# Shared value rows of an attention kernel: loaded once and copied on the chip, with one more load on a second DMA queue

## The chip, the cores and the metric

The kernel runs on one core of a Trainium2 chip. The metric is the device time of one execution in microseconds (us). All data are 32-bit floats.

The engines are named as in the profile: PE multiplies matrices (PEld is the loading of its weights), DVE works on vectors, ACT is the scalar engine, POOL is GpSimd, and SP issues DMAs. Each engine runs its instructions in the order of the program, and waits for others only through semaphores.

## The reference

Two parts follow each other. The first is chunked attention with memory: 4 batches, 8 heads, 768 positions, head size 64. Each chunk of 32 queries looks at 64 keys: 8 memory rows, 16 to the left, the 32 of the chunk and 8 to the right.

```python
for c in range(nc):                                  # 24 chunks of 32
    k_full = concat([mem_k, k[:, :, l_start:r_end]]) # 8 + up to 56 rows
    v_full = concat([mem_v, v[:, :, l_start:r_end]])
    scores = scale * q_c @ k_full.T
    a = exp(scores - max(scores)); a = a / (sum(a) + 1e-9)
    out[:, :, c_start:c_end] = a @ v_full
```

The second is a soft mixture of experts on the 3072 rows x of 512 numbers that come out: `logits = x @ phi` (32 slots, 4 for each of 8 experts); a softmax down the rows makes 32 slot inputs from x; each expert computes `relu(slot @ w1[e]) @ w2[e]`, with 2 MB of w1 and 2 MB of w2; and a softmax along the slots combines the 32 results into each row.

## The kernel before

**Tiles.** 128 positions, or 4 chunks, make a step u (24 of them), and two steps make a unit n (12 units, `NUNIT`). For a unit three things are loaded: q(n), 512 KB, and k(n), two transfers of 312 KB, into one of two slabs `kq0`, `kq1`; and v(n) into one of two slabs `v0`, `v1`. Heads go in pairs: the even partitions of k and v hold the first head of a pair, the odd ones the second (`par` in the code), and zeros stand in the halves of a slab that belong to the other head. For values the 64 rows that a chunk sees stand under each other, two partitions a row; a slab has one region for the first chunk of each two (`o` = 0) and one for the second (`o` = 1). The windows of the two chunks share 32 of their 64 rows, and these are loaded twice: v(n) is two transfers of 512 KB.

**A unit on PE.** The loop over n issues for each unit: transposes of the exponentials (`pt_ps`), the scores of the unit after it (`s`), logits (`l`) or transposes for the experts' softmax (`dt_ps`) in turn, a transpose of finished rows (`xt_ps`), the values of both steps (`a`), another `xt_ps`, and in each second unit `D_ps`, the slot sums. DVE and ACT do the softmax between `s` and `pt_ps`, ACT copies `pt`, `xT` and `dT` out of PSUM.

**The loads.** All DMAs are issued by SP, in order. In iteration n come q(n+3) and k(n+3) (when the scores that used the slab are done), then v(n+2) (when the values of unit n are done), then pieces of the experts' weights: 32 pieces of 1 MB, called w(0) to w(31) here. Twelve slabs `w0` to `w11` take the first twelve; further pieces go into kq, v and x slabs as the attention gives these up, and the last twelve into `w0` to `w11` again, each when PE has used the piece of w1 before it. `load_w(upto)` issues pieces up to a count; `n + 2` is the count in iteration n, and 11 from iteration 8.

**Semaphores of DMAs.** The layer that records the program gives each DMA one of eight semaphores, DMAHW0 to DMAHW7, in turn. A DMA waits until the DMA that had its semaphore before has landed. No more than eight DMAs are therefore on their way.

**After the attention** PE runs the eight experts' first product (`h`), then the second (`so`) in two blocks of 256 columns; each block is summed (`r`), combined into rows (`o`) and stored by six DMAs of 512 KB.

A small class sends every instruction through one helper, so that the profile shows L61 for nearly all of them; they are told apart by their tiles.

Of the kernel before, what the change touches and what calls it, by code (L numbers as in the profile page):

```python
# [16 lines left out]
P = 128  # L17
B, H, S, D = 4, 8, 768, 64
NPAIR = H // 2
CHUNK, LEFT, RIGHT, NMEM = 32, 16, 8, 8  # L20
NKEY = NMEM + LEFT + CHUNK + RIGHT
CPU = P // CHUNK
STEP = NMEM + 2 * CHUNK
UPB = S // P
NU = B * UPB
UU = 2
NUNIT = NU // UU
UNITS_B = UPB // UU
PAIRS = UU * CPU // 2
KW = PAIRS * STEP + LEFT + RIGHT  # L30
KB = NPAIR * KW
QW = UU * NPAIR * P
VB = UU * 2 * NPAIR * D
# [11 lines left out]
NEG = -1.0e30  # L45
PIECE = 2048
NW = 12
NIN = 2
# [18 lines left out]
def tile_attn_softmoe(  # L67
# [2 lines left out]
    qT: bass.AP,  # L70
    kT: bass.AP,
    vw: bass.AP,
    phi: bass.AP,
    w1: bass.AP,
    w2: bass.AP,
# [3 lines left out]
    pe, dve, act, sp, pool = (InOrder(tc, e) for e in (nc.tensor, nc.vector, nc.scalar, nc.sync, nc.gpsimd))  # L79
# [4 lines left out]
    kq_slab = [cp.tile([P, 2 * KB + QW], F32, tag=f"kq{i}", name=f"kq{i}") for i in range(NIN)]  # L84
# [8 lines left out]
    phi_sb = cp.tile([P, NKC, NSLOT], F32, tag="phi", name="phi_sb")  # L93
    warm = cp.tile([P, P], F32, tag="warm", name="warm")

    k_in = [t[:, 0:2 * KB].rearrange("p (a g n) -> p a g n", a=2, g=NPAIR) for t in kq_slab]
    q_in = [t[:, 2 * KB:].rearrange("p (u g n) -> p u g n", u=UU, g=NPAIR) for t in kq_slab]
    v_in = [t.rearrange("p a o (u c g d) -> p a o u c g d", u=UU, c=2, g=NPAIR) for t in v_slab]

# [8 lines left out]
    def load_kq(n):  # L108
        load_q(n)
        load_k(n)  # L110

    def load_v(n):
        t = v_slab[n % NIN]
        for par in range(2):
            sp.dma_start(t[par:P:2, par], vw[n, par])

    slabs = list(w_slab)
    usable = {i: NW for i in range(NUNIT + 2)}
# [15 lines left out]
    def load_w(upto):  # L134
        for i in range(len(where), min(upto, len(pieces))):
            kind, *at = pieces[i]
            where[pieces[i]] = s = slabs[i % len(slabs)]
            if kind == "w1":
                src = w1[at[0]].rearrange("(p kc) f -> p kc f", kc=NKC)[:, 2 * at[1]:2 * at[1] + 2, :]
                sp.dma_start(s.rearrange("p (k f) -> p k f", k=2), src)  # L140
            else:
                sp.dma_start(s, w2[at[0], at[1]])
# [12 lines left out]
    for i in range(NIN):  # L155
# [3 lines left out]
        out=kq_slab[1][:, 0:KB].rearrange("p (o n) -> p o n", n=104),  # L159
        in_=warm[:, 0:104].rearrange("p (o n) -> p o n", o=1).broadcast_to([P, KB // 104, 104]),  # L160
# [3 lines left out]
    for i in range(40):  # L164
        j = i % 4
# [15 lines left out]

    def scores(u):
        n, uu = divmod(u, UU)
        k, q = k_in[n % NIN], q_in[n % NIN]
        s_ps = ps.tile([P, H, NKEY], F32, tag="S", name=f"s{u}", bufs=2)
        for g in range(NPAIR):
            for j in range(CPU):
                w0 = (2 * uu + j // 2) * STEP + CHUNK * (j % 2)
                win = k[:, :, g, w0:w0 + NKEY]
                pe.matmul(  # L190
                    s_ps[32 * j:32 * j + 32, 2 * g:2 * g + 2, :],
                    lhsT=q[:, uu, g, 32 * j:32 * j + 32], rhs=win, start=True, stop=True,
                )
        return s_ps

    def softmax(u, s_ps):
        n, uu = divmod(u, UU)
        if u % UPB == 0:
            dve.memset(s_ps[0:32, :, 0:LEFT], NEG)
        if u % UPB == UPB - 1:  # L200
            dve.memset(s_ps[96:128, :, NKEY - RIGHT:NKEY], NEG)
        mx = wk.tile([P, H, 1], F32, tag="mx", name=f"mx{u}")
        dve.tensor_reduce(out=mx[:, :, 0], in_=s_ps, axis=AX.X, op=ALU.max)
        if uu == 0:
            pexp[n] = wk.tile([P, UU, NPAIR, NKEY, 2], F32, tag="p", name=f"p{n}")
        dve.tensor_tensor(
            out=pexp[n][:, uu].rearrange("p g n h -> p g h n"),
            in0=s_ps.rearrange("p (g h) n -> p g h n", h=2),
            in1=mx.rearrange("p (g h) o -> p g h o", h=2).broadcast_to([P, NPAIR, 2, NKEY]),
            op=ALU.subtract,  # L210
        )
        act.activation(out=pexp[n][:, uu], in_=pexp[n][:, uu], func=AF.Exp, scale=SCALE)

    def normalizer(n):
        z = wk.tile([P, UU, H], F32, tag="z", name=f"z{n}")
        zf = z.rearrange("p u h -> p (u h)")
        dve.tensor_reduce(
            out=z.rearrange("p u (g h) -> p (u g) h", h=2),
            in_=pexp[n].rearrange("p u g n h -> p (u g) h n"), axis=AX.X, op=ALU.add
        )  # L220
        dve.tensor_scalar_add(zf, zf, 1e-9)
        dve.reciprocal(out=zf, in_=zf)
        rz[n] = z

    def transpose_p(u):
        n, uu = divmod(u, UU)
        t_ps = ps.tile([P, NPAIR, P], F32, tag="T", name=f"pt_ps{u}", bufs=2)
        for g in range(NPAIR):
            pe.transpose(t_ps[:, g, :], pexp[n][:, uu, g].rearrange("p n h -> p (n h)"), ident)
        pt = wk.tile([P, NPAIR, P], F32, tag="pt", name=f"pt{u}", bufs=2)  # L230
        act.copy(out=pt, in_=t_ps)
        return pt
# [15 lines left out]
    def normalize(u, a_ps):  # L248
        n, uu = divmod(u, UU)
        dve.tensor_tensor(  # L250
            out=x_slab[u // 4 % 2][:, u % 4, :].rearrange("p (h d) -> p h d", d=D), in0=a_ps,
            in1=rz[n][:, uu].rearrange("p (h o) -> p h o", o=1).broadcast_to([P, H, D]), op=ALU.mult,
        )
# [103 lines left out]
    for u in range(UU):  # L357
        softmax(u, scores(u))
# [3 lines left out]
    for n in range(NUNIT):  # L362
        us = (2 * n, 2 * n + 1)
        last = n + 1 == NUNIT
        Gl = (n - 3) // 2 if n >= 3 and n % 2 == 1 else None
        Gd = (n - 4) // 2 if n >= 4 and n % 2 == 0 else None
        pts = [transpose_p(u) for u in us]
        if n >= 1:
            for u in us:
                normalize(u - 2, a_ps[u - 2])  # L370
        normalizer(n)
        if not last:
            s_ps = [scores(u + 2) for u in us]
        if n + 3 < NUNIT:
            load_kq(n + 3)
        if Gd is not None:
            dispatch_t(Gd)
        if Gl is not None:
            l_ps = logits(Gl)
        if n >= 1:  # L380
            transpose_x(us[0] - 2)
        if not last:
            for u, t in zip(us, s_ps):
                softmax(u + 2, t)
        if Gd is not None:
            combine_exp(Gd)
        if Gl is not None:
            dispatch_max(Gl, l_ps)
            dispatch_lT(Gl, l_ps)
            dispatch_exp(Gl, l_ps)  # L390
            if Gl >= 1:
                combine_div(Gl - 1)
        a_ps[us[0]] = values(us[0], pts[0])
        if last:
            transpose_x(us[1] - 2)
            normalize(us[0], a_ps[us[0]])
            dispatch_t(NG - 2)
        a_ps[us[1]] = values(us[1], pts[1])
        if n >= 1 and not last:
            transpose_x(us[1] - 2)  # L400
        if Gd is not None:
            D_ps = dispatch(Gd)
            dispatch_z(Gd)
            dispatch_sum(Gd, D_ps)
        if n + 2 < NUNIT:
            load_v(n + 2)
        load_w(usable[n] if n >= NUNIT - 3 else n + 2 + (n == NUNIT - 4))

    normalize(NU - 1, a_ps[NU - 1])
    transpose_x(NU - 2)  # L410
# [161 lines left out]
    sh = slot_out(0)  # L572
# [6 lines left out]
def _layouts(inputs):  # L579
    q, k, v = inputs["q"], inputs["k"], inputs["v"]  # L580

    def stream(x, mem):
        half = CHUNK // 2
        parts = [np.zeros((B, H, LEFT, D), x.dtype), x[:, :, :half]]
        for t in range(half, S, 2 * CHUNK):
            parts += [mem, x[:, :, t:t + 2 * CHUNK]]
        parts.append(np.zeros((B, H, RIGHT, D), x.dtype))
        return np.concatenate(parts, axis=2)

    qT = q.reshape(B, NPAIR, 2, UNITS_B, UU, P, D).transpose(0, 3, 6, 2, 4, 1, 5).reshape(NUNIT, P, QW)  # L590
    ks = stream(k, inputs["mem_k"])
    cols = np.array([[t * PAIRS * STEP + c for c in range(KW)] for t in range(UNITS_B)])
    kT = ks[:, :, cols].reshape(B, NPAIR, 2, UNITS_B, KW, D).transpose(0, 3, 2, 5, 1, 4).reshape(NUNIT, 2, D, KB)

    vs = stream(v, inputs["mem_v"])

    rows = np.array([[STEP * i + CHUNK * o + r for o in range(2) for r in range(NKEY)] for i in range(S // (2 * CHUNK))])
    vw = vs[:, :, rows].reshape(B, NPAIR, 2, UNITS_B, UU, 2, 2, NKEY, D).transpose(0, 3, 2, 7, 6, 4, 5, 1, 8)
    vw = vw.reshape(NUNIT, 2, NKEY, 2, VB)
    w2 = inputs["moe_w2"].reshape(E, NFC, P, NBLK, WB).transpose(3, 0, 2, 1, 4).reshape(NBLK, E, P, NFC * WB)  # L600
    return {"qT": qT, "kT": kT, "vw": vw, "phi": inputs["moe_phi"], "w1": inputs["moe_w1"], "w2": w2}


# [16 lines left out]
```

## Time and profile before

| | |
|---|---|
| time, median of 3 runs | 169.67 us (168.94 to 170.69) |
| the profiled execution | 170.3 us, of which the span of its instructions is 168.5 us |
| mean granted PE clock | 0.975 |
| PE, DVE, ACT, POOL busy | 139.9, 99.5, 60.4, 8.5 us |
| DMA packets | 66.84 MB, mean 397 GB/s |

The page lists for each engine how long it was busy, the span in 40 slices, the DMA queues, and the chain of work that ended last. The chain is followed back from the end: each row is a piece of work or a transfer that the next one waited for. In the list of waits a row names the engine and tile that waited, what released it, and the total, the number and the longest wait. "issue" there stands for a wait that the profile can't put down to any instruction or transfer.

### The profile page before, as it was taken

The numbers are of one execution on the slowest core, as the hardware profiler recorded it, in microseconds if no ns is written. First come the engines' busy times: TensorE is split into PE (matmuls) and PEld (weight loads), VectorE is DVE, ScalarE is ACT, GpSimd is POOL, SyncE is SP. The second block draws the span as 40 slices with busy tenths as digits, with TensorE's granted clock in tenths as the row PEclk, the third lists the DMA queues.
The fourth block names the chain that finished last, engine by engine and source line by source line (L and its number), as shares of the span: only waits on it lengthen the run. The fifth ranks groups of instructions, "written<-read, shape, count | busy, mean of one in ns | idle before, by whom it ended". The sixth has DMA issues, their size and how long they took to land.

```text
span 168.5 us, 6123 instructions
## 1 busy us (share of the span) xinstructions
PE 139.9 (83%) x2729; PEld 102.1 (61%) x2729; DVE 99.5 (59%) x216; ACT 60.4 (36%) x129; POOL 8.5 (5%) x13
## 2 busy tenths in 40 slices
PE   7369997895979979995995998889999999887800
PEld 6257885784758866884684766647655565553500
DVE  6566997974929994999498949466300101081620
ACT  5023543714532734371535455431122100070520
POOL 8700000000000000000000202000000000000000
PEclk9995999999999999999999999999999999999995
DMA  5999999999999999999999999999999999999896
GB/s 205 360 387 416 404 375 379 424 424 416 413 425 412 422 415 414 419 413 421 414 417 396 321 364 420 426 408 422 418 422 416 424 416 422 416 404 399 350 407 240
DMA packets 12458, 66.84 MB, mean 397 GB/s; under 512 B 2193, under 2 KB 2193, under 8 KB 6801
## 3 DMA queue, kind: packets, MB, share of 16 engines
q1 hardware_dynamic: 12432, 66.46, 97.1%
q8 instruction: 21, 0.34, 0.8%
q14 instruction: 5, 0.03, 0.0%
HBM read 60.16 MB, written 6.29 MB: 394 GB/s over the span
## 4 chain that ended last, share of the span: by engine, by line
PE 55%; DMA 22%; DVE 7%; issue 6%; POOL 3%; ACT 2%; DVEq 0%; ACTq 0%; POOLq 0%
PE s L61 13%; DMA w<-in_w_dram 12%; PE a L61 10%; PE xt_ps L61 6%; DMA kq<-in_kT_dram 6%; PE h L61 5%; PE pt_ps L61 4%; DMA kq<-in_qT_dram 4%; PE o L61 3%; PE D_ps L61 3%; PE l L61 3%; PE so L61 2%; POOL v L61 2%; PE dt_ps L61 2%; DVE v L61 1%
## 5 line engine op out<-in xcount | busy, mean ns | idle before, releaser
L61 PE MATMUL s<-kq 128*32 128x128 f32 x768 | 27.8, 294 | 6.7 <-issue 3.0
L61 PE MATMUL a<-v,pt 128*32 128x128 f32 x768 | 25.0, 274 | 4.9 <-issue 4.9
L61 PEld LDWEIGHTS s<-kq 128*32 128x32 f32 x768 | 23.1, 119 | 8.3 <-issue 4.9
L61 PEld LDWEIGHTS a<-v,pt 128*32 128x32 f32 x768 | 20.6, 110 | 8.0 <-issue 7.7
L61 ACT COPY xT<-xt_ps 128x512 f32<-128x512 f32 (+1 forms) x24 | 13.8, 576 | 28.4 <-PE xt_ps L61 28.4
L61 ACT ACTIVATE p<-p 128x512 f32<-128x512 f32 x24 | 14.7, 630 | 15.9 <-DVE p L61 15.9
L61 DVE TENSOR_TENSOR x<-a,z 128x512 f32<-128x512 f32 x24 | 15.6, 683 | 3.8 <-PE a L61 3.8
L61 DVE TENSOR_REDUCE mx<-s 128x8 f32<-128x512 f32 x24 | 16.3, 678 | 2.7 <-PE s L61 2.4
L61 DVE TENSOR_TENSOR p<-s,mx 128x512 f32<-128x512 f32 x24 | 16.7, 695 | 0.8
L61 PE MATMUL xt_ps<-ident,x 128*128 128x128 f32 x96 | 15.5, 284 | 0.0
L61 ACT COPY pt<-pt_ps 128x512 f32<-128x512 f32 x24 | 13.0, 590 | 5.5 <-PE pt_ps L61 5.5
L61 DVE TENSOR_REDUCE z<-p 128x16 f32<-128x1024 f32 x12 | 14.5, 1212 | 0.7 <-ACT p L61 0.7
L61 PE MATMUL pt_ps<-ident,p 128*128 128x128 f32 x96 | 13.3, 279 | 1.9 <-issue 1.2
L61 PEld LDWEIGHTS pt_ps<-ident,p 128*128 128x128 f32 x96 | 10.6, 141 | 6.0 <-ACT xT L61 3.4
L61 PEld LDWEIGHTS xt_ps<-ident,x 128*128 128x128 f32 x96 | 10.2, 140 | 4.0 <-issue 2.8
L61 PE MATMUL so<-w,hT 128*32 128x256 f32 x192 | 11.4, 381 | 0.5 <-DMA w<-in_w_dram 0.5
L61 PE MATMUL h<-w,siT 128*32 128x256 f32 x192 | 10.8, 380 | 0.1
L61 PE MATMUL o<-sh,cst 32*128 32x256 f32 x96 | 8.0, 404 | 1.6 <-DVE kq L61 0.6
L61 PEld LDWEIGHTS so<-w,hT 128*32 128x32 f32 x192 | 5.8, 110 | 5.5 <-DMA w<-in_w_dram 1.4
L61 DVE COPY hT<-ht_ps 128x32 f32<-128x32 f32 x8 | 1.2, 186 | 13.3 <-PE ht_ps L61 8.6
L61 PEld LDWEIGHTS h<-w,siT 128*32 128x32 f32 x192 | 6.0, 110 | 4.2 <-DVE siT L61 0.3
L61 PEld LDWEIGHTS o<-sh,cst 32*128 32x128 f32 x96 | 5.3, 184 | 4.3 <-DVE kq L61 1.4
(94 smaller groups left out, 133.5 us busy)
## 6 DMA issues: line engine op xcount, KB each, us to landing
w<-in_w_dram SPq DMA_DIRECT2D x24, 1024.0 KB, 11.8
v<-in_vw_dram SPq DMA_DIRECT2D x24, 512.0 KB, 9.3
kq<-in_kT_dram SPq DMA_DIRECT2D x24, 312.0 KB, 9.3
kq<-in_qT_dram SPq DMA_DIRECT2D x12, 512.0 KB, 9.6
v<-in_w_dram SPq DMA_DIRECT2D x4, 1024.0 KB, 9.8
out_dram<-v SPq DMA_DIRECT2D x8, 512.0 KB, 5.1
kq<-in_w_dram SPq DMA_DIRECT2D x2, 1024.0 KB, 10.1
x<-in_w_dram SPq DMA_DIRECT2D x2, 1024.0 KB, 8.5
```

Source lines behind the costliest of these rows:

```text
L61: return self.tc.keep_in_program_order(f(*args, **kwargs))
```

## The change

`load_v(n)` loads the rows of the first region alone (two transfers of 256 KB, `vw`), and for the second region only the 32 rows that are new (two transfers of 128 KB, `vx`). The new rows of the first head go on SP's queue, those of the second head on ACT's. The 32 shared rows are copied by POOL from the first region to the second, 64 partitions by 1024 numbers for each head. A copy stays on its partitions, so the order of the 64 keys in a chunk's window changes: for the second chunk the two halves of 32 are swapped, and the second head of a pair holds its keys in reverse, so that its shared rows lie in the other half of the partitions. The scores' matmul reads its keys through patterns that fit (two strides instead of one for second chunks), the masks of batch edges are set per head (two DVE memsets in place of one), and the order of rows on the host's side follows.

From iteration 4 on `load_w` goes one piece further than before, up to iteration 8, where both have issued 11.

```diff
     def load_v(n):
         t = v_slab[n % NIN]
         for par in range(2):
-            sp.dma_start(t[par:P:2, par], vw[n, par])
+            sp.dma_start(t[par:P:2, par, 0], vw[n, par])
+        for par in range(2):
+            (sp, act)[par].dma_start(t[65 * par:65 * par + 63:2, par, 1], vx[n, par])
+        for par in range(2):
+            shared = slice(64, P) if par == 0 else slice(0, 64)
+            pool.tensor_copy(out=t[shared, par, 1], in_=t[shared, par, 0])
...
     def scores(u):
...
-                win = k[:, :, g, w0:w0 + NKEY]
+                win = key_window(n, g, w0)
+                if j % 2:
+                    win = win.rearrange("p a (t i) -> p a t i", t=2)[:, :, ::-1, :]
...
     def softmax(u, s_ps):
         n, uu = divmod(u, UU)
+        sh = s_ps.rearrange("p (g h) n -> p g h n", h=2)
         if u % UPB == 0:
-            dve.memset(s_ps[0:32, :, 0:LEFT], NEG)
+            dve.memset(sh[0:32, :, 0, 0:LEFT], NEG)
+            dve.memset(sh[0:32, :, 1, NKEY - LEFT:NKEY], NEG)
...
-        load_w(usable[n] if n >= NUNIT - 3 else n + 2 + (n == NUNIT - 4))
+        load_w(usable[n] if n >= NUNIT - 3 else n + 2 + (n >= 4))
```

Below, V(n) stands for the two `vw` transfers of unit n, X(n) for the `vx` transfer on SP and A(n) for the one on ACT. With them a unit issues eight DMAs, and the semaphores fall to others than before. Three places of the program show what moved.

**SP in iteration 5** (q(8) and k(8) into kq0, v(7) into v1, then w). Before:

```order
L61 DMA kq0_64<-in_qT_dram 128x1024 [waits DMAHW5_49,PE_49]
L61 DMA kq0_64<-in_kT_dram 64x1248 [waits DMAHW6_49]
L61 DMA kq0_64<-in_kT_dram 64x1248 [waits DMAHW7_49]
L61 DMA v1_67<-in_vw_dram 64x2048 [waits DMAHW0_49,PE_49]
L61 DMA v1_67<-in_vw_dram 64x2048 [waits DMAHW1_49]
L61 DMA w6_76<-in_w1_dram 128x2048 [waits DMAHW2_49]
```

And now:

```order
L61 DMA kq0_64<-in_qT_dram 128x1024 [waits DMAHW6_49,PE_49]
L61 DMA kq0_64<-in_kT_dram 64x1248 [waits DMAHW7_49]
L61 DMA kq0_64<-in_kT_dram 64x1248 [waits DMAHW0_49]
L61 DMA v1_67<-in_vw_dram 64x1024 [waits DMAHW1_49,PE_49,Pool_49]
L61 DMA v1_67<-in_vw_dram 64x1024 [waits DMAHW2_49,Pool_49]
L61 DMA v1_67<-in_vx_dram 32x1024 [waits DMAHW3_49,PE_49]
L61 DMA w7_77<-in_w1_dram 128x2048 [waits DMAHW4_49]
```

The q(8) transfer has DMAHW6 now, which A(7) had before it. A(7) is issued by ACT at the end of this same iteration. In the same way q(9) follows A(8) in iteration 6, V(2) follows A(2) and V(3) follows A(3).

**ACT at the end of iteration 5** (xT9 is its copy of the last `xt_ps` of the iteration, pt12 and pt13 belong to the next):

```order
L61 COPY xT9_996<-xt_ps9_991 128x512 [waits PE_49]
L61 DMA v1_67<-in_vx_dram 32x1024 [waits DMAHW6_49]
L61 COPY pt12_1010<-pt_ps12_1005 128x512 [waits PE_49,Activation_49]
L61 COPY pt13_1017<-pt_ps13_1012 128x512 [waits PE_49,Activation_49]
L61 COPY dT1_1065<-dt_ps1_1062 128x128 [waits PE_49]
```

The DMA row, A(7), is new; what stands before and behind it stood there before. The semaphore that it waits for was A(6)'s.

**SP at iteration 9**, the last v load, v(11), and the first weights behind it. Before:

```order
L61 DMA v1_67<-in_vw_dram 64x2048 [waits DMAHW6_49,PE_49]
L61 DMA v1_67<-in_vw_dram 64x2048 [waits DMAHW7_49]
L61 DMA w11_81<-in_w1_dram 128x2048 [waits DMAHW0_49]
L61 DMA kq0_64<-in_w1_dram 128x2048 [waits DMAHW1_49]
L61 DMA kq1_65<-in_w1_dram 128x2048 [waits DMAHW2_49,PE_49]
```

And now:

```order
L61 DMA v1_67<-in_vw_dram 64x1024 [waits DMAHW5_49,PE_49,Pool_49]
L61 DMA v1_67<-in_vw_dram 64x1024 [waits DMAHW6_49,Pool_49]
L61 DMA v1_67<-in_vx_dram 32x1024 [waits DMAHW7_49,PE_49]
L61 DMA w11_81<-in_w1_dram 128x2048 [waits DMAHW0_49]
L61 DMA kq0_64<-in_w1_dram 128x2048 [waits DMAHW1_49]
L61 DMA kq1_65<-in_w1_dram 128x2048 [waits DMAHW2_49,PE_49]
```

X(11) has DMAHW7, which A(11) had before it; w(11) and all weights stand behind X(11) on SP.

More of the change, by code (lines that the diff above doesn't have):

```diff
@@ L72, in tile_attn_softmoe @@
     vw: bass.AP,
+    vx: bass.AP,
     phi: bass.AP,
@@ L94, in tile_attn_softmoe @@
     warm = cp.tile([P, P], F32, tag="warm", name="warm")
-    k_in = [t[:, 0:2 * KB].rearrange("p (a g n) -> p a g n", a=2, g=NPAIR) for t in kq_slab]
     q_in = [t[:, 2 * KB:].rearrange("p (u g n) -> p u g n", u=UU, g=NPAIR) for t in kq_slab]
@@ L114, in load_v, with key_window @@
         for par in range(2):
-            sp.dma_start(t[par:P:2, par], vw[n, par])
+            sp.dma_start(t[par:P:2, par, 0], vw[n, par])
[4 more added lines that the diff above has]
+            pool.tensor_copy(out=t[shared, par, 1], in_=t[shared, par, 0])
+    def key_window(n, g, w0):
+        t = kq_slab[n % NIN]
+        keys = t[:, g * KW + w0:g * KW + w0 + NKEY]
+        step = KB + KW - NKEY - 2 * w0
+        part, (one, count) = keys.ap[0], keys.ap[-1]
+        return bass.AP(tensor=keys.tensor, offset=keys.offset, ap=[part, [step, 2], [one, count]])
     slabs = list(w_slab)
@@ L183, in scores @@
         n, uu = divmod(u, UU)
-        k, q = k_in[n % NIN], q_in[n % NIN]
+        q = q_in[n % NIN]
         s_ps = ps.tile([P, H, NKEY], F32, tag="S", name=f"s{u}", bufs=2)
@@ L197, in softmax @@
         n, uu = divmod(u, UU)
+        sh = s_ps.rearrange("p (g h) n -> p g h n", h=2)
         if u % UPB == 0:
-            dve.memset(s_ps[0:32, :, 0:LEFT], NEG)
+            dve.memset(sh[0:32, :, 0, 0:LEFT], NEG)
+            dve.memset(sh[0:32, :, 1, NKEY - LEFT:NKEY], NEG)
         if u % UPB == UPB - 1:
-            dve.memset(s_ps[96:128, :, NKEY - RIGHT:NKEY], NEG)
+            dve.memset(sh[96:128, :, 0, CHUNK - RIGHT:CHUNK], NEG)
+            dve.memset(sh[96:128, :, 1, CHUNK:CHUNK + RIGHT], NEG)
         mx = wk.tile([P, H, 1], F32, tag="mx", name=f"mx{u}")
@@ L592, in _layouts, with rows @@
     cols = np.array([[t * PAIRS * STEP + c for c in range(KW)] for t in range(UNITS_B)])
-    kT = ks[:, :, cols].reshape(B, NPAIR, 2, UNITS_B, KW, D).transpose(0, 3, 2, 5, 1, 4).reshape(NUNIT, 2, D, KB)
+    kT = ks[:, :, cols].reshape(B, NPAIR, 2, UNITS_B, KW, D).transpose(0, 3, 2, 5, 1, 4)
+    kT = np.stack([kT[:, :, 0], kT[:, :, 1, :, :, ::-1]], axis=2).reshape(NUNIT, 2, D, KB)
     vs = stream(v, inputs["mem_v"])
-    rows = np.array([[STEP * i + CHUNK * o + r for o in range(2) for r in range(NKEY)] for i in range(S // (2 * CHUNK))])
-    vw = vs[:, :, rows].reshape(B, NPAIR, 2, UNITS_B, UU, 2, 2, NKEY, D).transpose(0, 3, 2, 7, 6, 4, 5, 1, 8)
-    vw = vw.reshape(NUNIT, 2, NKEY, 2, VB)
+    def rows(first, count):
+        r = np.arange(first, first + count)
+        at = np.array([[STEP * i + r, STEP * i + r[::-1]] for i in range(S // (2 * CHUNK))])
+        w = vs.reshape(B, NPAIR, 2, -1, D)
+        w = np.stack([w[:, :, par][:, :, at[:, par]] for par in range(2)], axis=2)
+        w = w.reshape(B, NPAIR, 2, UNITS_B, UU, 2, count, D).transpose(0, 3, 2, 6, 4, 5, 1, 7)
+        return w.reshape(NUNIT, 2, count, VB)
+    vw, vx = rows(0, 2 * CHUNK), rows(2 * CHUNK, CHUNK)
     w2 = inputs["moe_w2"].reshape(E, NFC, P, NBLK, WB).transpose(3, 0, 2, 1, 4).reshape(NBLK, E, P, NFC * WB)
-    return {"qT": qT, "kT": kT, "vw": vw, "phi": inputs["moe_phi"], "w1": inputs["moe_w1"], "w2": w2}
+    return {"qT": qT, "kT": kT, "vw": vw, "vx": vx, "phi": inputs["moe_phi"], "w1": inputs["moe_w1"], "w2": w2}
 def kernel(**inputs):
```

## The prediction

> **What bounds the kernel now.** The page's engine row, slices and queues come first.
>
> ```profile
> PE 139.9 (83%) x2729; PEld 102.1 (61%) x2729; DVE 99.5 (59%) x216; ACT 60.4 (36%) x129; POOL 8.5 (5%) x13
> DMA  5999999999999999999999999999999999999896
> q1 hardware_dynamic: 12432, 66.46, 97.1%
> ```
>
> The DMA engines look like the bound: 97% of the span, nine tenths or more in nearly every slice. But a full queue delays nothing unless somebody waits for what is in it. So the second view is the list of what PE waited for (engine, tile, releaser; total us, times, longest).
>
> ```profile
> PE a L61 <- issue: 4.9, 4, 1.8
> PE s L61 <- issue: 3.0, 3, 1.3
> PE s L61 <- DMA kq<-in_kT_dram: 0.7, 1, 0.7
> PE so L61 <- DMA w<-in_w_dram: 0.5, 1, 0.5
> ```
>
> PE waits for DMA twice, 1.2 us in all; 7.9 us of its stops have no releaser. The chain that ended last (start, us, what) shows where the two are.
>
> ```profile
> 23.46 9.96 DMA kq<-in_kT_dram
> ...
> 33.56 2.12 PE s L61 x63
> ...
> 125.23 20.04 DMA w<-in_w_dram
> 145.31 1.07 PE so L61 x16
> ```
>
> One is k(4), landing at 33.4, the other a weight at 145.3. Between them the chain runs on PE or in the short exchange of DVE, ACT and PE after the last unit. So from 33 us on the attention goes at PE's pace, and loads keep just ahead. Two stretches (length, busy time of PE, PEld, DVE, ACT, POOL, clock, DMA share, GB/s) give the pace of both:
>
> ```profile
> 51.30:58.40 7.10, 6.96 (x180) 5.96 (x184) 6.70 (x18) 3.37 (x9) 0.00 (x0) 1.00 1.02 418
> 125.20:145.30 20.10, 19.35 (x319) 10.97 (x311) 1.29 (x7) 1.93 (x4) 0.00 (x0) 1.00 1.01 419
> ```
>
> PE is busy for 6.96 of 7.10 and 19.35 of 20.10 us, and at 418 GB/s a piece of 1 MB takes 2.5 us. **PE and DMA are bounds at once**, so taking work from one of them buys only what the other was waiting for it.
>
> **The part removed.** Each v(n) shrinks from 1024 to 768 KB: 12 x 262 kB = 3.15 MB, or 7.5 us of DMA at 418 GB/s. Of that, the path gets what PE waited for. v(0), v(1), v(2) stand ahead of k(4), 0.79 MB or 1.9 us, more than the wait of 0.66 us: **the wait for k(4) goes, -0.66**. What is next there is PE itself.
>
> The other end is the tail. Issues by SP (start, us, what), and landings of single issues (count, KB, us from issue to landing): w(11) issued at 93.45; the last weight, w(31), at 132.5 (the twelfth of its row, which ends at 132.88); the first out of the second block, at 158.16; and the last two outs.
>
> ```profile
> 92.29 1.12 SPq L61 DMA_DIRECT2D v<-in_vw_dram  x2
> 93.45 1.57 SPq L61 DMA_DIRECT2D w<-in_w_dram  x1
> 117.49 15.39 SPq L61 DMA_DIRECT2D w<-in_w_dram  x12
> 158.16 5.40 SPq L61 DMA_DIRECT2D out_dram<-v  x6
> w<-in_w_dram SPq DMA_DIRECT2D x1, 1024.0 KB, 8.2
> w<-in_w_dram SPq DMA_DIRECT2D x1, 1024.0 KB, 20.1
> out_dram<-v SPq DMA_DIRECT2D x1, 512.0 KB, 3.2
> out_dram<-v SPq DMA_DIRECT2D x2, 512.0 KB, 5.2
> ```
>
> w(11) landed at 101.65, w(31) at 152.65: 20 pieces in 51.0 us, 2.55 each, so this queue never ran dry. Twelve outs of 1.25 us follow: 152.65 + 15 = 167.6, the landing of the last (162.4 + 5.2). The end of the kernel is thus tied to when w(11) starts moving, which is when SP is let through at iteration 9.
>
> **The wait added.** There X(11) waits for A(11)'s landing, with all weights behind it on SP. A(11) follows ACT's copy of `xT`, whose rows in iterations 9 and 5 are
>
> ```profile
> 92.88 0.59 ACT L61 COPY xT<-xt_ps 128x512 f32<-128x512 f32 x1 [1.70 <-PE xt_ps L61]
> 58.05 0.57 ACT L61 COPY xT<-xt_ps 128x512 f32<-128x512 f32 x1
> ```
>
> No DMA of ACT's stands in this trace, so its time from issue to landing, L, is bounded. The out above took 3.2 us with 1.25 of bytes, so 1.95 is fixed; 128 KB add 0.31: L = 2.3 at the least. The v row below gives 5.8 for a load behind a full queue. I take 2.3: ACT's queue holds nothing else, and with 0.26 MB less in each unit SP's has run down by then.
>
> ```profile
> v<-in_vw_dram SPq DMA_DIRECT2D x2, 512.0 KB, 5.8
> L61 SPq DMA_DIRECT2D v<-in_vw_dram x24: 471/562/1193, 4.8 to 92.8; - x24
> ```
>
> A(11) starts at 93.47, lands at 95.8; X(11) takes 0.5 to issue (median 562 ns); w(11) goes at 96.3 instead of 93.45. In an empty queue it lands 1.95 + 2.5 later, at 100.75: 0.9 before 101.65, and with PE's 0.66, 1.55 earlier. w(31) then lands at 151.1, and the weight that PE waited for at 145.3 is there in time: -0.48 more on PE. The second block's outs start 0.66 + 0.48 = 1.14 earlier, at 157.0; the first lands 3.2 later, five more of 1.25 behind it: 166.45 instead of 167.6. **Both ends give -1.1.**
>
> [...]
>
> **The same wait in earlier iterations.** q(8) waits for A(7), and with it k(8) and v(7) behind it. The rows are q(8)'s issue, and starts of PE work on units 5 to 9:
>
> ```profile
> 53.61 0.33 SPq L61 DMA_DIRECT2D kq<-in_qT_dram  x1
> ...
> 55.04 1.88 PE a L61 x64
> 62.80 1.88 PE a L61 x64
> 67.86 1.88 PE s L61 x64
> 71.20 0.56 PE a L61 x12
> 75.22 1.88 PE s L61 x63
> ```
>
> Values of unit 5 end at 56.92; A(7) can start at 58.62 and lands at 60.9, so q(8) is issued 7.3 us late. It lands 3.2 later, k(8) 1.5 after that: 65.7, and the scores that need it start at 67.86: 2.2 to spare. q(9) behind A(8), one unit on (64.68 + 1.7 + 2.3 + 4.7 = 73.4), has 1.8 before 75.22. V(2) behind A(2) goes about 3 us late, lands by 25.5 and is copied by 28.3; its values start at 29.49, as the last row below says. V(3) likewise has time. So this costs nothing as long as L stays under about 4, and 1 us per us above.
>
> **The part added on POOL.** Two copies of 64 x 1024 a unit. The rows near it:
>
> ```profile
> L61 POOL MEMSET v<- 128x2048 f32 x2 | 3.5, 1806 | 0.0
> L61 DVE MEMSET v<- 128x2048 f32 x2 | 3.5, 1765 | 0.8 <-issue 0.8
> L61 POOL MEMSET hT<- 128x1024 f32 x2 | 2.0, 976 | 95.7 <-DVE z L61 95.7
> L61 POOL COPY gsum<-sel 128x128 f32<-128x128 f32 x1 | 0.3, 291 | 0.0
> 29.49 1.96 PE L61 MATMUL a<-v,pt 128*32 128x128 f32 x64
> ```
>
> At the memset's pace a copy takes 1.0 us, at eight times the 128x128 copy 2.3. I take 1.4, nearer to the row of that size; two are 2.8, one may be over before the last load lands. v(7): V lands behind k(8) by 67.0, the first half at 66.4; copied at 69.2, or 71.0 at the dear end; needed at 71.20. Cost 0; at the dear end some 0.2 for v(2).
>
> **Small parts.** ACT issues 12 DMAs of about 0.5 us, 6 us of its time. Behind each stand the copies of `pt`; those in the row below end at 59.60 for values at 62.80, so I cost it at 0; without that cover it is 0.5 a unit, 6 in all. DVE's masks go from one memset of 165 ns to two of 112 at the left edge, and from one of 112 to at most two such at the right; only the one at u = 0 is on the path: +0.06.
>
> ```profile
> 58.52 1.08 ACT L61 COPY pt<-pt_ps 128x512 f32<-128x512 f32 x2
> L61 DVE MEMSET s<- 32x128 f32 x4 | 0.7, 165 | 3.8 <-PE s L61 3.6
> L61 DVE MEMSET s<- 32x64 f32 x4 | 0.4, 112 | 0.3
> ```
>
> Keys read through two strides: between 0 and an allowance of 5% on twelve runs of 1.9 us, 1.2 us; I take 0, since runs of `s` and of `a` with their different patterns both take 1.88. X and A write 32 partitions each; at half the rate they would take 0.3 us more, which only the tail feels. Weights one piece ahead in iterations 4 to 7: 0, as both have 11 by iteration 8, and of the weights PE waits for the one at 145.3 alone.
>
> **Sum.** -0.66 - 0.48 + 0.06 = -1.1, rounded to -1.0 for the tail's small items. Against the profiled execution (170.3) that is 169.3; this one was 0.6 above the median, so **168.7** against 169.67. About 1% is what a measurement of this kernel can tell from no change.
>
> **Rivals.**
> - *The bytes count in full*: PE stretches with DMA everywhere; -7.5 us, 162.2. For it: 97% DMA. Against it: 1.2 us of waits in all. Chance 0.04.
> - *PE's stops without a releaser shrink.* They fall within runs of equal matmuls, where no semaphore is waited for, and the page has a queue for instructions that runs on the same engines. If the stops are fetches that a full queue draws out, fewer bytes shorten them. Half of 7.9 us is -4 more: 164.7. In proportion to the bytes of a unit (8% less), -0.6. Chance of the large form 0.16.
>
> ```profile
> q8 instruction: 21, 0.34, 0.8%
> ```
>
> - *SP stands behind ACT* (slower). If L is over 4, because ACT's transfer gets through as slowly as SP's own, or ACT comes late to issue it, the empty queue at 93 us is paid for in full. At 5.8, q(8) is 1.3 late, q(9) 1.7, w(11) 3.5 more: PE +2.3, the end +4.9: 174.6. Chance 0.11. A smaller form, L near 4, leaves nothing of the gain: 169.7, chance 0.08.
> - *POOL's copies and DVE slow each other.* In the row 51.30:58.40 DVE has 0.4 us to spare. If 2 us of copies held up DVE for as long, that is 1.6 a unit in six such units: +9.6, 178. Against it: two memsets of 128x2048 on DVE and POOL lay side by side at 1765 and 1806 ns, no slower per number than POOL's 976 for half of it. [...] Chance 0.05.
>
> **How the numbers follow.** The forecast has 0.56, within 168 and 171 by the small parts' bounds. Range 165.4 to 172.2: it takes in most of the stops' rival and the light half of ACT's, and leaves out 162.2, 174.6 and 178. Faster by over 1% (under 168.0): 0.04 + 0.14 + 0.07 of the forecast's lower edge = 0.25. Slower (over 171.4): 0.10 + 0.05 + 0.02 = 0.17. Within: 0.58.
>
> **What would show it.** Right: no wait of `s` for kq at 33 us, none of `so` for w; DMA share clearly under 1 in the attention; A landing in 2 to 3 us; q(8) issued near 61 and SP idle ahead of w(11); copies of 1.0 to 1.7 us; PE's runs as long as before. Wrong: waits of `a` for POOL, of `s` for kq at units 8 and 9, or stops that change by more than 2 us in total.

## The result and the profile after

The changed kernel takes **185.53 us** (median of 4 runs, 183.92 to 186.69) against 170.18 (168.94 to 171.58) in the same comparison: a ratio of 1.090, 95% interval 1.073 to 1.106. The forecast was 168.7, with a range that ended at 172.2. The profiled execution is the one of 183.92 us; its span is 182.1 us, its mean PE clock 0.944. Here and below, medians are of all runs, while ratios leave out runs more than 1.5% above the fastest of the same kernel (below, six of the ten of e8, and three of the four of e10, which has no ratio for that reason), so that a ratio can lie under what the medians give.

The page's engine row, rate in slices and queues:

```profile
PE 142.6 (78%) x2729; PEld 104.5 (57%) x2729; DVE 102.8 (56%) x224; ACT 61.0 (33%) x129; POOL 33.4 (18%) x37
DMA  6998979999999986999999947999999999999896
GB/s 213 372 272 283 379 232 312 407 365 367 383 342 352 343 315 203 299 391 362 345 346 375 302 157 268 360 418 430 428 412 418 427 414 418 425 419 408 366 410 258
q1 hardware_dynamic: 13008, 61.74, 90.6%
q10 hardware_dynamic: 576, 1.57, 2.8%
```

The bytes went down as planned, from 66.84 to 63.70 MB. But in 18 of the first 25 slices, in the attention, the DMA engines are still shown busy for nine tenths or more, while they mostly move 300 to 380 GB/s; behind them, where weights move, they are back near 420. The same stretch of 60 us in both kernels (length, busy time of PE, PEld, DVE, ACT, POOL, PE clock, DMA share, GB/s), before and then after:

```profile
40.00:100.00 60.00, 53.38 (x1175) 41.71 (x1175) 46.79 (x102) 27.88 (x63) 0.97 (x1) 1.00 1.00 405
```

```profile
40.00:100.00 60.00, 48.14 (x1002) 38.16 (x995) 41.03 (x88) 23.30 (x52) 12.88 (x13) 0.94 0.97 342
```

The engines' share fell from 1.00 to 0.97, the rate by 16%: most of it went because the engines moved less while they were busy, a smaller part because the queue was empty. What PE waited for shows the two again:

```profile
PE s L61 <- DMA kq<-in_kT_dram: 10.1, 4, 3.4
PE a L61 <- issue: 5.8, 5, 1.8
PE s L61 <- issue: 4.7, 3, 2.2
PE so L61 <- DMA w<-in_w_dram: 2.2, 2, 1.4
```

Of the 10.1 us for kq, 2.9 are at the very start, which was there before too (put down to `gsum` then). The other 7.2 are k(3), k(4) and k(8), against 0.7 for k(4) before: +6.5. `so` has +1.7, the stops without a releaser (with `pt_ps` 11.4 against 9.1) +2.3, and PE is busy 2.7 longer, with a mean granted clock of 0.944 against 0.975. That is 13.2 of the span's 13.6 us.

SP's own list of waits has a row that was not there:

```profile
SPq L61 <- DMA v<-in_vx_dram: 24.0, 7, 8.9
```

Seven times, for 24.0 us together, SP stood behind a vx transfer. Four of these waits make 23.0 us: 6.6 ahead of V(2), 8.9 ahead of q(8), 4.0 ahead of q(9) and 3.5 ahead of X(11), the loads that stand behind A(2), A(7), A(8) and A(11) on ACT's queue. In the chain that ended last the dearest place is iteration 5, where A(7) was to let q(8) through:

```profile
62.64 6.39 DMA v<-in_vx_dram
...
69.09 0.33 SPq L61
...
70.02 5.91 DMA kq<-in_kT_dram
...
75.97 3.21 PE s L61 x64
```

A(7) takes 6.39 us from issue to landing, q(8) is issued at 69.09 instead of 53.61, k(8) lands at 75.9, and the scores of one step then take 3.21 us instead of 1.88 (from 75.9 to 79.2 us the granted clock is 0.59). While SP stood, its queue ran dry: between 67 and 70 us the DMA engines were busy a quarter of the time (share, then GB/s, at the end of the row):

```profile
67.00:70.00 3.00, 2.65 (x65) 2.08 (x61) 2.69 (x7) 1.77 (x5) 0.00 (x0) 1.00 0.24 83
```

So there are two suspects, and POOL's copies are a third. **Theory 1**: SP stands behind ACT's transfer at shared semaphores. **Theory 2**: the vx transfers write only one half of the partitions each, and this slows the DMA engines. **Theory 3**: POOL's copies, by latency or contention. The runs below tell them apart; all times are medians, beside a kernel before of 169.8 to 170.2 us.

### The profile page after: what moved, and what is told of

Same layout as the page of the kernel before. It is cut to its first block, busy times and chain, and to the rows that moved or that the text cites. A ratio compares the mean times of both kernels' runs of the same rounds, so it can differ in the third digit from the quotient of the medians.

```text
span 182.1 us, 6245 instructions
## 1 busy us (share of the span) xinstructions
PE 142.6 (78%) x2729; PEld 104.5 (57%) x2729; DVE 102.8 (56%) x224; ACT 61.0 (33%) x129; POOL 33.4 (18%) x37
## 2 busy tenths in 40 slices
DMA packets 13610, 63.70 MB, mean 350 GB/s; under 512 B 2576, under 2 KB 2576, under 8 KB 9488
## 4 chain that ended last, share of the span: by engine, by line
PE 48%; DMA 30%; DVE 7%; issue 6%; ACT 2%; SPq 2%; POOL 1%; DVEq 0%; ACTq 0%; POOLq 0%
DMA kq<-in_kT_dram 15%; PE s L61 11%; DMA w<-in_w_dram 11%; PE a L61 9%; PE h L61 5%; PE xt_ps L61 5%; DMA v<-in_vx_dram 4%; PE pt_ps L61 3%; PE o L61 3%; PE l L61 3%; PE D_ps L61 2%; PE so L61 2%; SPq L61 2%; PE dt_ps L61 1%; DVE v L61 1%
## 5 line engine op out<-in xcount | busy, mean ns | idle before, releaser
L61 POOL COPY v<-v 64x1024 f32<-64x1024 f32 x24 | 25.0, 1040 | 78.5 <-DMA v<-in_vw_dram 67.9
L61 PE MATMUL s<-kq 128*32 128x128 f32 x768 | 27.6, 295 | 14.8 <-DMA kq<-in_kT_dram 10.1
L61 PE MATMUL a<-v,pt 128*32 128x128 f32 x768 | 26.3, 282 | 6.5 <-issue 5.8
L61 PEld LDWEIGHTS a<-v,pt 128*32 128x32 f32 x768 | 21.5, 113 | 10.1 <-issue 8.4
L61 PE MATMUL xt_ps<-ident,x 128*128 128x128 f32 x96 | 16.0, 290 | 0.0
L61 PE MATMUL pt_ps<-ident,p 128*128 128x128 f32 x96 | 14.1, 289 | 1.4 <-issue 0.9
L61 PEld LDWEIGHTS pt_ps<-ident,p 128*128 128x128 f32 x96 | 11.1, 147 | 6.0 <-ACT xT L61 3.4
L61 PE MATMUL so<-w,hT 128*32 128x256 f32 x192 | 11.4, 381 | 2.2 <-DMA w<-in_w_dram 2.2
```

Of the source, the lines that this page charges most:

```text
L61: return self.tc.keep_in_program_order(f(*args, **kwargs))
```

## The experiments

| version | A(n) on | new rows go to | copies | load_w | us (runs) | ratio to before, 95% |
|---|---|---|---|---|---|---|
| after | ACT | halves | yes | ahead | 185.5 (4) | 1.073 to 1.106 |
| e5 | ACT | halves | yes | as before | 184.9 (4) | 1.068 to 1.091 |
| e1 | SP | halves | yes | ahead | 180.2 (4) | 1.047 to 1.067 |
| e2 | POOL | halves | yes | ahead | 180.0 (4) | 1.049 to 1.065 |
| e7 | SP | halves | no | ahead | 179.6 (4) | 1.051 to 1.062 |
| e13 | SP | middle half | yes | ahead | 176.6 (4) | 1.028 to 1.047 |
| e8 | SP | all partitions | yes | ahead | 171.0 (10) | 0.991 to 1.003 |
| e10 | SP | all partitions | yes | as before | 171.5 (4) | none |
| e11 | ACT | all partitions | yes | ahead | 180.2 (4) | 1.045 to 1.065 |
| e12 | POOL | all partitions | yes | ahead | 171.5 (10) | 0.998 to 1.008 |
| e3 | whole region on SP | | no | ahead | 172.8 (4) | 1.010 to 1.029 |
| e6 | whole region on SP | | yes | ahead | 173.9 (5) | 1.020 to 1.028 |
| e9 | whole region on SP | | no | as before | 170.5 (10) | 0.997 to 1.006 |
| e4 | the kernel before | | | ahead | 170.5 (10) | 1.002 to 1.010 |

**e1: everything on SP.**

```diff
-            (sp, act)[par].dma_start(t[65 * par:65 * par + 63:2, par, 1], vx[n, par])
+            sp.dma_start(t[65 * par:65 * par + 63:2, par, 1], vx[n, par])
```

> The changed kernel with A(n) on SP's queue instead of ACT's; bytes, copies and key order stay. Theory 1 (SP stands behind ACT's transfer at shared semaphores): 167 to 170 us, since nothing on SP waits for ACT any more; SP's waits ahead of v go from 8.9 us to under 2, PE's waits of s for kq from 10.1 to under 2. Theory 2 (transfers into a half of the partitions, and more of them, run the DMA engines slower): 178 to 184, the DMA rate in the attention stays near 350 GB/s with the share near 1. Theory 3 (POOL's copies, by their latency or by contention): 181 to 186, PE's waits of a for POOL stay and DVE's slowed operations too.

180.2: a third of the loss is gone, and two thirds stay. SP's waits for vx are down to 0.7 us, as theory 1 had it, but the rate in the stretch 40 to 100 us is no better (341 GB/s at a share of 1.02). Theory 1 is part of the cause and, beside the halves, not the larger part.

**e2: A(n) issued by POOL.** `(sp, pool)[par]` in the same place.

> The changed kernel with A(n) issued by POOL, ahead of its copies, instead of ACT. A second queue stays, but it has semaphores of its own, so no load of SP waits for it. Theory 1: 167 to 171 us, as with all on SP. Theory 2: 178 to 186, because half of the partitions and the second queue both stay. Theory 3: 181 to 188.

180.0, the same as e1. Here a second queue is no better or worse than one, once SP doesn't wait for it.

**e3, e6, e9: the second region loaded whole.** The bytes of before in four transfers of 64 partitions each; in e6 the copies on top of that; in e9 load_w as before.

```diff
         for par in range(2):
-            (sp, act)[par].dma_start(t[65 * par:65 * par + 63:2, par, 1], vx[n, par])
-        for par in range(2):
-            shared = slice(64, P) if par == 0 else slice(0, 64)
-            pool.tensor_copy(out=t[shared, par, 1], in_=t[shared, par, 0])
+            sp.dma_start(t[par:P:2, par, 1], vx[n, par])
...
```

> The changed kernel with the second region loaded whole on SP (two transfers of 256 KB, 64 partitions each) and no copies on POOL: the bytes of the kernel before in four transfers instead of two, in the new order of keys, with load_w as changed. All theories: 169 to 172 us, since neither ACT's queue, nor transfers into half of the partitions, nor copies are left. If it is over 174, the key order, the number of transfers or load_w's schedule cost by themselves, and no theory so far has that.

> The second region loaded whole on SP, and POOL's copies on top of it (they write the same rows again once these have landed). The copies' cost by themselves, with the bytes of the kernel before. Theory 2 (transfers into a half of the partitions slow the DMA engines): 171 to 175 us, as without the copies (172.8), DMA packets at their usual pace. Theory 3 (POOL's copies slow the DMA engines, or PE waits for them): 177 to 183.

> The second region loaded whole on SP, no copies, load_w's schedule as before. Against the kernel before only the number of v transfers (four of 256 KB) and the order of keys remain. If the weight one piece ahead was what made the version with the changed load_w 2.8 us slower than before: 169 to 171 us. If the number of transfers or the key order was: 172 to 174.

e3 came to 172.8, above the 172 expected. e9 puts that down to load_w's schedule: with the old one 170.5, the time of the kernel before, so the order of keys and the number of transfers are free. e6 is 1.1 above e3, with intervals that overlap: the copies cost about 1 us, and no more than 3 by the ends of the intervals. Theory 3 falls.

**e4 and e5: load_w's line alone.** e4 is the kernel before with `n + 2 + (n >= 4)`, e5 the changed kernel with `n + 2 + (n == NUNIT - 4)`.

> The kernel before with only the change of load_w: one weight piece earlier in iterations 4 to 7. If it costs in itself (more bytes ahead of q and k just where both engines are full): 172 to 174 us, with new waits of s for kq around units 7 to 9. If it was priced rightly at nothing: 169 to 171.

> The changed kernel with load_w's schedule as before (no piece ahead from iteration 4). The semaphores shift by one from iteration 4 on, so that other loads of SP wait for A(n). Theory 1: 175 to 190 us, depending on which loads those are: q no longer waits for A in iterations 5 and 6. Theories 2 and 3: 183 to 187, the schedule of one weight moves little.

e4 is slower by 0.2 to 1.0%; e5 can't be told from the changed kernel. A weight one piece ahead costs some 1 us where all bytes are loaded (2 between e9 and e3), and is not what this change lost by. In e5's profile SP stood behind vx for 12.2 us instead of 24.0, but `s` waited 9.6 us for kq, nearly as long as the 10.1 of the changed kernel: what counts is which loads stand, not the sum.

**e7 and e8: the halves by themselves.** e7 is e1 without the two lines of the copies. e8 keeps e1's bytes and packets and spreads each vx transfer over every fourth of 128 partitions. Its copies have the same size, but both write into the second head's part and both vx transfers into the first head's, so the values of second chunks are not the reference's (in e10 to e13 too):

```diff
-            sp.dma_start(t[65 * par:65 * par + 63:2, par, 1], vx[n, par])
+            sp.dma_start(t[2 * par:P:4, 0, 1], vx[n, par])
...
-            pool.tensor_copy(out=t[shared, par, 1], in_=t[shared, par, 0])
+            pool.tensor_copy(out=t[shared, 1, 1], in_=t[shared, par, 0])
```

> The changed kernel with both vx transfers on SP and without POOL's copies; the shared rows of the second region are left out, so the result lacks them. Theory 2: 178 to 181 us, as with the copies (180.2), with packets of 8 KB at 340 ns in the mean or more. Theory 3: 169 to 173, with packets of 8 KB near 318 ns.

> The changed kernel with both vx transfers on SP, of the same bytes and packets, but each spread over every fourth partition of all 128 instead of every second one of a half (both into the region of the first head, both copies into that of the second, so the values of the second chunk of each two are not those of the reference). Theory 2: 169 to 173 us, packets of 8 KB near 318 ns, rate above 380 GB/s in the attention. Theory 3: 178 to 182, as with the halves.

179.6 without copies, 171.0 with the rows spread: **the halves cost 9 us**, whatever the copies do. Where PE lost it is in the list of its waits, of e7 and then of e8:

```profile
PE s L61 <- issue: 9.7, 6, 2.4
PE a L61 <- issue: 5.1, 4, 2.0
```

```profile
PE a L61 <- issue: 3.9, 3, 2.0
PE s L61 <- DMA kq<-in_kT_dram: 3.0, 1, 3.0
PE s L61 <- issue: 2.1, 3, 1.1
```

Not in waits for a load, but in stops within `s` and `a` that no semaphore ends: 14.8 us against 6.0, in one profile each. The other profiles agree: 16.5 in e1 and 11.9 in e2, but 5.3 to 9.1 in the kernel before and in e3, e4, e6, e9, e10 and e12, which have neither halves nor ACT's queue.

The traces tell what PE stops for. On the page's queue q8, of kind `instruction`, 21 packets of 16 KB arrive, and PE runs 2729 matmuls with as many weight loads: 260 to a packet, or 130 matmuls with their weight loads. From the 345th matmul on, the stops of over 0.2 us lie at nearly the same places in all of these kernels, some 126 matmuls apart (one of 0.6 us in the changed kernel lies elsewhere), and where PE stops at such a place for over 0.3 us, the next matmul starts 1.2 to 1.7 us after the end of such a packet (110 stops in fifteen kernels). One place, in the chain of the kernel before and in that of e1:

```profile
90.09 1.76 issue
91.85 0.41 PE a L61 x3
```

```profile
100.00 3.71 issue
103.71 0.42 PE a L61 x7
```

The packet on q8 ran from 89.43 to 90.54 us in the kernel before, and from 101.21 to 102.44 in e1. So **PE stops for its instructions**. From one such place to the start of the next packet it takes 3.75 to 4.00 us in the mean (eleven places) in the kernel before and in e3, e4, e6, e8, e9, e10 and e12, but 4.55 to 4.84 in e1, e2 and e7. That the packet stands among the loads on the same DMA engines meanwhile is argued from this; no run shows it by itself.

**e10: spread, with load_w as before.**

> As the version with the new rows spread over all partitions, both on SP (the values of the second chunk of each two are again not those of the reference), with load_w's schedule as before: what the saved bytes and the copies are worth when nothing else of the change is left. The prediction's sum without its terms for ACT's queue: 168.5 to 170 us. If DMA had been the bound, 163 to 166. If the copies cost something by themselves: 171 to 173.

171.5 (168.3 to 173.1). With the halves, ACT's queue and load_w's line gone, the 3.1 MB less are worth nothing that these runs can measure. Where they went can be seen in e8, which differs from e10 by load_w alone, between 90 and 92 us (the kernel before, then e8):

```profile
90.00:92.00 2.00, 0.24 (x5) 0.14 (x2) 1.86 (x8) 1.18 (x4) 0.00 (x0) 1.00 0.98 406
```

```profile
90.00:92.00 2.00, 0.23 (x7) 0.15 (x7) 1.70 (x7) 0.94 (x4) 0.00 (x0) 1.00 0.04 8
```

The queue has run dry. SP stands until PE is done with the slab that v(11) goes into, and issues v(11) at 92.27 us, against 92.29 before. In e12 it is the same: 16 GB/s in that stretch, and v(11) at 92.39.

**e11 and e12: ACT's queue by itself.** e8 with A(n) on ACT, and with A(n) on POOL, where the pair below is `(sp, pool)`.

```diff
-            sp.dma_start(t[2 * par:P:4, 0, 1], vx[n, par])
+            (sp, act)[par].dma_start(t[2 * par:P:4, 0, 1], vx[n, par])
```

> The new rows spread over all partitions, as before without the right values in the second chunks, but with A(n) on ACT's queue and load_w as changed: everything of the change except the halves. If standing behind ACT costs by itself: 174 to 177 us, A(n) landing 4 to 7 us after its issue. If A(n) was late only because the DMA engines were slow and full: 170 to 172 us, A(n) landing in 2 to 4 us.

> The new rows spread over all partitions (values of the second chunks as in the other spread versions), with A(n) issued by POOL ahead of its copies: a second queue, but semaphores of its own. If the price of ACT's queue (171.0 without it, 180.2 with it) is SP's standing at shared semaphores: 170 to 172.5 us, though A(n) lands late here too. If it is the second queue as such: 177 to 182.

e11 is at 180.2, worse than its first theory's 174 to 177: with the DMA engines near e8's pace (362 GB/s at a share of 0.96 from 40 to 100 us, against 369 at 0.93), **ACT's queue costs 9 us too**. e12, with a queue as slow as ACT's (POOLq's row is from e12, ACTq's from e11), is at 171.5:

```profile
v<-in_vx_dram ACTq DMA_DIRECT2D x12, 128.0 KB, 5.9
```

```profile
v<-in_vx_dram POOLq DMA_DIRECT2D x12, 128.0 KB, 5.6
```

Both land late; only e11 makes SP wait. Its lists for SP and PE:

```profile
SPq L61 <- DMA v<-in_vx_dram: 31.0, 7, 7.4
```

```profile
PE s L61 <- DMA kq<-in_kT_dram: 13.6, 6, 3.0
```

So the price is SP's standing at semaphores that it shares with ACT. (e12 takes the issuing itself off ACT too, but PE's waits for ACT are the same in e11 as in e8, row by row.) It stood 31.0 us, k came late five times (the sixth wait is the one at the start), and PE's stops without a releaser in `s` and `a` shrank to 2.1 us: while PE waits for k, its instructions arrive. At the 596th matmul, where PE comes at 38.17 us after a wait for k, the packet had ended 4.7 us earlier. The two causes don't add up (9 and 9 over e8, together 14.5), which fits this: one wait covers the other.

**m2: how long ACT's transfer takes.** Its edit is a kernel of transfers only.

> Transfers alone: loads of 128 KB on an empty chip, two on ACT's queue and two on SP's; then SP loads of 1 MB (8 KB packets) in a row with four loads of 128 KB on ACT's queue at intervals, spread over every fourth partition; the same with these on the even ones of the lower 64; SP loads of 256 KB (4 KB packets) with four on ACT; and SP loads of 2 MB and of 4 MB in all with one on ACT behind them. If ACT's transfer passes SP's backlog, as the prediction took it: 2 to 2.6 us from issue to landing everywhere. If it waits for what SP has queued: about 2 us empty, and then with the backlog, 5 to 8 us behind 2 MB and more.

The issues of three stretches (count, KB, us to landing): alone on the chip; behind 1 MB loads of SP, spread over all partitions; the same into the lower half.

```profile
s<-in_vx_dram ACTq DMA_DIRECT2D x2, 128.0 KB, 2.4
...
s<-in_vx_dram ACTq DMA_DIRECT2D x4, 128.0 KB, 5.6
...
b<-in_w_dram SPq DMA_DIRECT2D x5, 1024.0 KB, 15.4
s<-in_vx_dram ACTq DMA_DIRECT2D x4, 128.0 KB, 6.4
```

2.4 us on an empty chip, 5.6 with SP's backlog beside it, 6.4 if it writes a half. It passes most of that backlog (SP's own loads take 13.4 and 15.4 us there), and yet does not come down to the 2.3 that the prediction took: 3.2 us are added to those of the empty chip. What they consist of no run shows. In the other groups it takes 2.3 to 4.6 us behind loads of 256 KB, whose queue ran dry in between, and 3.9 and 6.3 behind 2 and 4 MB.

**m1, m3, e13: which partitions are slow.** m1 and m3 are transfers alone; e13 is e8 with the new rows in partitions 32 to 95.

> Transfers alone, nothing of the attention: eleven groups of 16 loads of 256 KB in 4 KB packets, in this order: every fourth partition of 128; the even ones of the lower 64; these and the odd ones of the upper 64 in turn; the same two with the second on ACT's queue; every fourth partition on both queues; the first 32; the first 32 and the third 32 in turn; every second of 128; the lower 64; every fourth with POOL's copies beside; two of every second partition and two of the halves in turn. Theory 2: the groups on a half run at half to three quarters of the rate of the first (near 418 GB/s), those on 32 neighbours slower still, and halves in turn gain part of it back. Otherwise all groups run alike, and the slow packets in the kernel come from something that goes on beside them.

Windows inside nine of the groups of m1 (DMA share and GB/s at the end). In order: the even partitions of the lower 64; halves in turn; halves on two queues; the first 32; the first and the third 32 in turn; every second of 128; the lower 64; every fourth; two of every second and two halves in turn.

```profile
33.00:49.00 16.00, 1.46 (x14) 0.00 (x0) 1.00 1.03 203
51.00:62.00 11.00, 0.89 (x8) 0.00 (x0) 1.00 1.04 279
66.00:81.00 15.00, 1.04 (x10) 0.00 (x0) 1.00 1.01 238
97.00:115.00 18.00, 1.46 (x14) 0.00 (x0) 1.00 1.04 203
117.00:131.00 14.00, 1.25 (x12) 0.00 (x0) 1.00 1.04 256
133.00:140.80 7.80, 1.04 (x10) 0.00 (x0) 1.00 1.03 418
145.00:162.00 17.00, 1.25 (x12) 0.00 (x0) 1.00 1.04 207
165.00:170.00 5.00, 0.34 (x4) 0.00 (x0) 1.00 1.03 392
177.00:190.00 13.00, 1.46 (x14) 0.00 (x0) 1.00 1.03 260
```

The share is 1 everywhere, the rate is not: 203 and 207 GB/s into the lower half against 418 into every second of all, and the first 32 partitions, at 203, are as fast as 64 of the same half. (The copies meant for the group on every fourth ran at 19 to 28 us, beside the first two groups, so the group says nothing on them.)

> The new rows in the middle half, partitions 32 to 95 (even ones by one transfer, odd ones by the other, both on SP; both copies go into the region of the second head, so the values of the second chunks are not those of the reference). Same bytes and packets as with the lower and upper halves (180.2 us) and as spread over all (171.0). [...] If any half is slow: 178 to 181.

> Transfers alone again, 256 KB in 4 KB packets on SP, nothing of the attention: the even partitions of the middle half (32 to 95); these and the odd ones in turn; then, in fours, two loads over all 128 partitions (every second one) and two of another kind: over every fourth of 128, in the middle half, in the lower and the upper half in turn. If the middle half reaches all ways into the memory: 418 GB/s for it alone, and the three mixes tell what is lost beside others: over 400 for every fourth, 260 as measured for lower and upper halves, the middle between if other loads get in its way. If any half is slow: near 205 for the middle alone.

e13 took 176.6, between the spread rows (171.0) and the halves (180.2). The windows of m3: the middle half, its even and odd partitions in turn, then the mixes of full loads with every fourth, with the middle, and with lower and upper halves:

```profile
26.00:47.00 21.00, 1.39 (x14) 0.00 (x0) 1.00 1.03 276
49.00:70.00 21.00, 1.30 (x12) 0.00 (x0) 1.00 1.04 277
77.00:89.00 12.00, 1.04 (x10) 0.00 (x0) 1.00 1.03 417
94.00:113.00 19.00, 1.46 (x14) 0.00 (x0) 1.00 1.04 282
117.00:134.00 17.00, 0.42 (x4) 0.00 (x0) 1.00 1.04 243
```

The middle half reaches 277 GB/s by itself: faster than the lower (203), slower than all (418). What limits it no run here shows. The order of the rates alone, 418, 277 and 203, is that of the kernels' times, 171.0, 176.6 and 180.2.

## Why the prediction was wrong, point by point

- **L, the time of A(n)**: the first step that failed. 2.3 us is right for an empty chip (2.4 measured) and was taken for a full one; measured in the changed kernel:

```profile
v<-in_vw_dram SPq DMA_DIRECT2D x24, 256.0 KB, 6.7
...
v<-in_vx_dram ACTq DMA_DIRECT2D x12, 128.0 KB, 6.3
v<-in_vx_dram SPq DMA_DIRECT2D x12, 128.0 KB, 7.2
```

  "SP's has run down by then" did not hold (a DMA share of 0.97 from 40 to 100 us). The upper bound, 5.8 from the row of v, was the better one, though that row is v(11), ahead of which SP had stood for 5.9 us, and so no load behind a full queue: all v loads of the kernel before have a median of 9.3. A(7) also left later than the forecast had it, at 62.64 us instead of 58.62, as PE was late by then. The rival built on that bound (174.6) had the right mechanism at half its price: it charged q(8), q(9) and w(11) with 4.9 us, and left out V(2), behind which k(4) came late, and V(3), ahead of which SP stood 6.5 us in e11. e11 puts it at 9.
- **"At half the rate they would take 0.3 us more, which only the tail feels"**: the second step that failed, and as large. The half rate was right (203 against 418). But 0.3 us on each of two transfers was taken for the whole price, and for one that nobody else pays. In m1, halves in turn run at 279 GB/s by themselves; with as many full loads at 418 between them that would make 335, and the mix runs at 260 (243 in m3). Charged to the halves alone, 260 means 0.76 us more for the 256 KB of a unit than at 418, or 9.1 us over 12 units. From e8 to e1 it is 9, in a stretch where the DMA engines had no time to spare (a share of 1.02 in e1), and PE pays it at its stops for instructions (6.0 us in `s` and `a` in e8, 16.5 in e1). The text itself said that DMA was a bound; it then priced a slower DMA as if it weren't.
- **The k(4) wait goes (-0.66), and the weight's (-0.48)**: neither did; they grew by 6.5 and 1.7. In e8, e10 and e12, where nothing delays the loads, the gain can't be seen either (171.0 to 171.5). The wait for k(4) is gone in their profiles, but it is in e4's too, which loads all bytes. The tail's gain began as forecast and was lost on the way: in e12 w(11) lands at 100.6 us (forecast 100.75, before 101.65), but the weight that `so` waits for lands at 145.7, against 145.3 before.
- **That saved bytes are worth little** held: bytes in full (162.2) is refuted by e8 and e10.
- **PE's stops without a releaser shrink** (164.7): that they are waits for instructions, which this rival supposed, the traces bear out. Fewer bytes did not shorten them clearly (7.9 us in `s` and `a` before, 6.0 to 7.7 in e8, e10 and e12), and halves drew them out (11.9 to 16.5 in e1, e2 and e7).
- **The copies**: 1.4 us forecast, near the low bound in fact. DVE's large operations kept their times (the row of `p` was 695 ns before too, that of `mx` 678, and is 681 now); some of its small ones grew (the row of `z` was 175 ns before, and is again in e7, without copies; `c` times `cz` took 292 before and takes 388). `a` waited for POOL once, for 0.7 us, one of the signs of being wrong that the prediction names. e6 prices all of it at about 1 us, so this rival (178) was rightly small.

```profile
L61 POOL COPY v<-v 64x1024 f32<-64x1024 f32 x24 | 25.0, 1040 | 78.5 <-DMA v<-in_vw_dram 67.9
L61 DVE TENSOR_SCALAR z<-z 128x16 f32<-128x16 f32 x12 | 3.8, 318 | 0.4
L61 DVE TENSOR_TENSOR p<-s,mx 128x512 f32<-128x512 f32 x24 | 16.7, 695 | 0.8
```

- **Key strides and masks at nothing** held (e9 at the time of before). **Weights ahead at nothing** was off by about 1 us (e4).

No version tried is faster than the kernel before. Of those with fewer bytes the spread rows come nearest, and they are a measurement, not a kernel, as they leave the right values of second chunks out.

## What to carry to other kernels

Where the DMA share is near 1, price a transfer by the rate of its own partitions and charge the loss to every load behind it: here 128 KB into one half of the partitions, at 203 GB/s into the lower against 418, was not a small transfer. Where PE stops inside a run of equal matmuls, look at the packets of the instruction queue: here the stops ended 1.2 to 1.7 us after one. Before a load moves to another engine's queue, list which loads on the first queue share a semaphore with it, and price their wait with the latency under backlog (here 5.6 to 6.4 us), not with the empty chip's 2.4. Saved bytes did not pay on this kernel, whose PE is as full as its DMA: the queue ran dry instead (8 GB/s from 90 to 92 us in e8).

## What the runs showed of the hardware that was not expected

- Loads of 4 KB packets ran at 418 GB/s into every second of 128 partitions, 277 into the middle 64, 203 to 207 into the lower 64 or the first 32, with the DMA engines shown as busy in each: at the same share, 1.03 or 1.04, the rate differed by a factor of two.
- A load of 128 KB on a second queue took 2.4 us on an empty chip and 5.6 with a backlog of 1 MB loads on the first.
- PE's stops without a releaser in `s` and `a` ranged from 2.1 us (e11) to 16.5 (e1), with the same instructions on PE. Those of over 0.3 us at the places 126 matmuls apart ended 1.2 to 1.7 us after the end of a 16 KB packet on the instruction queue.
